# Gated layer: the landing mark of x renamed, the output's weights loaded in two halves behind x

## The chip, the cores and the metric

One core of a Trainium2 chip runs the whole program. TensorE (PE) does the matmuls, ScalarE (ACT), VectorE (DVE) and GpSimd (Pool) the elementwise work, and SyncE (SP) issues the DMAs, all in one queue. The metric is the time of one launch in microseconds of the device, the median of the runs.

## The reference

Three layers follow each other on 4 batches of 576 positions and 512 channels: windowed attention, a feed-forward layer with ReLU ("expert layer" here), and a gated layer. The change lies in the gated layer:

```python
def _moe2_ref(x, w_in, g_ln, w_sg, b_sg, w_out) -> np.ndarray:
    h = x @ w_in
    h = 0.5 * h * (1.0 + np.tanh(c * (h + 0.044715 * h ** 3)))
    u, v = (h[..., :d_ff // 2], h[..., d_ff // 2:])
    ...
    v_n = (v - mu) / np.sqrt(var + 1e-06) * g_ln
    v_s = np.einsum('ts,bsd->btd', w_sg, v_n) + b_sg[None, :, None]
    gated = u * v_s
    return (x + gated @ w_out).astype(np.float32)
```

`w_in` is 512 x 1024, its two halves `wu` and `wv` in the kernel; `w_out` (`wo`) is 512 x 512 and `w_sg` (`ws`) 576 x 576. `w_in` and `w_out` come as 64-bit floats, `w_sg` as 32-bit ones.

## The kernel before

Every product is done in three matmul terms: each operand is split into a rounded part and a rest (`h` and `l`, type F32R), and high x high, low x high and high x low are added up in PSUM. A split (`split`) is one ACT copy, which rounds, and one subtraction on DVE or Pool. The gated layer runs from about 515 us. Its work is cut into **units**: `V`, `U` (the two halves of `x @ w_in`), `S` (the spatial product) for each of the 4 batches, a short unit for the last 64 positions of all batches (`Vt`, `Ut`, "the tail") and `O` for the output's product of each of 9 groups. The order of the units is V0, U0, Vt, V1, U1, V2, U2, V3, U3, Ut, S0, S1, O0, O1, S2, O2, O3, S3 and the other O. The text calls U0 the first U unit, and so on.

A unit of V, U or S multiplies 2 x 2 blocks with seven products of half size in place of eight (`CHAIN`, in the order 1, 2, 6, 5, 7, 3, 4), which needs sums and differences of the blocks ahead (`prep`, `add`; on DVE or Pool) and of the results behind. Behind products 1, 6 and 5 ACT copies PSUM to a tile `te` (`evac`, L1390); products 7 and 3 start only when the copy of 6 and of 5 is done. Behind products 2, 7 and 3 DVE adds PSUM to such a copy (`sum`, L1396); product 4 waits for the sum of 7. ACT's GELU (`use`, L1413) then empties the sum into `u` or `v`, and V's rows are normalized (`norm`: statistics L1429, L1432, L1433 on DVE, a power on Pool, the scaling L1441 on ACT). There are five `te` tiles.

The batches' x lie in DRAM (`x2d`) from the expert layer. `load_x(b)` loads two pieces `xf` of 512 KB each and lets `prep` split seven blocks `bX` from them; `load_tail` does the same for the tail. The 64-bit weights `wo` are loaded in four pieces of 512 KB (`f64`, kc 0 to 3, tile `st`, two of them), turned to 32 bits by one ACT step (L84) and four DVE steps (L89, L91, L93, L96, tile `sc`), and split into `woh` and `wol`. `w_late` does that, then loads and splits a remainder of `ws` (tiles `k`, `b`), then loads the rest of `ws` (tile `wf`) and mixes its blocks (`mixed`, tile `mx`), which overwrite those of `wv`.

The order on each engine is not written by hand. A planner (`Sched`) runs while the program is built: a step is an `Op` with an engine, a guessed duration, a priority and the marks (`need`) that must be set before it. A mark is a name in a table, `done`, with the time at which the planner thinks it set. The planner takes the step that can start first, the priority counted in, and writes its instructions; on the chip each engine then works through its own list in that order. The marks are not on the chip: there, waits follow from what an instruction reads and overwrites. The expert layer sets marks named ("xl", g, p) for its groups g and parts p (in `rest`), and the gated layer's loads set ("xl", b, j).

Of the kernel before, what the change touches and what calls it, by code (L numbers as in the profile page):

```python
# [985 lines left out]
class Phase2:  # L986
# [52 lines left out]
    def open_0(self, sched):  # L1039
# [24 lines left out]
        for b in range(1, B):  # L1064
            self.go(self.load_x(b))
        for z in (self.load_tail(), self.v_tail(), self.u_tail(), self.w_late(), self.finish()):
            self.go(z)
# [51 lines left out]
    def f64(self, w, src, kc):  # L1119
        pri = self.wpri(w) + kc  # L1120
        nd = [("room", "late"), ("xl", 1, 1)] if w == "wo" else []
        yield Op("SP", 500, pri, need=nd, slots=[("st2", 2, ("st2", w, kc))], token=("ld2", w, kc), size=2 ** 19)
# [136 lines left out]
    def load_x(self, b):  # L1259
        pri = self.pri("V", b, -50)  # L1260
        key = "X", b
        fs = []
        for j in range(2):
            nd = [("x2", 2 * b + j)] + ([("P", "V", b - 1, 2)] if b > 1 else [("P", "U", 0, 1)] if b else [])
            o = Op("SP", 500, pri + j, need=nd, take=[("X", 1, ("src", key, j))], token=("xl", b, j), size=2 ** 19)
            yield o
            fs.append(self.get(o.got[0], [128, 4, 256], F32, "xf"))
            self.nc.sync.dma_start(out=fs[j], in_=self.x2d[2 * b + j])
        v = fs[0][:, 0:2], fs[1][:, 0:2], fs[0][:, 2:4], fs[1][:, 2:4]
        if b == 1:  # L1270
            yield Op(None, 0, 0, need=[("b", ("X", B), n) for n in range(3)])
        yield from self.prep(key, v, 2, pri, [("xl", b, 0), ("xl", b, 1)])

# [6 lines left out]
    def load_tail(self):  # L1280
        pri = self.pri("Vt", 0, -50)
        key = "X", B
        o = Op("SP", 500, pri, need=[("x2", G - 1)], take=[("X", 1, ("src", key, 0))], token=("xl", B, 0),
               size=2 ** 19)
# [9 lines left out]
        for n in range(2):  # L1294
            self.go(block(n, x[:, 2 * n:2 * n + 2], [("xl", B, 0)], ("src", key, 0), 3))
        t = yield from self.add(lambda g: self.get(g[0], [128, 2, 256], F32, "tt"), x[:, 2:4], x[:, 0:2], ALU.subtract, 512, pri,
                                take=[("tt", 1, ("tt", key, 2))], need=[("xl", B, 0)])
        self.used(("src", key, 0), 3, self.last)
# [218 lines left out]
    def w_late(self):  # L1517
# [31 lines left out]
        S.done["bdf"] = S.done["bt"] = S.free[self.last] + HOP  # L1549
        pri = self.wpri("ws")  # L1550
        self.W["ws"] = self.W["wv"]
# [208 lines left out]
```

## Time and profile before

| what | value |
|---|---|
| median of 3 runs | 730.87 us (729.82 to 731.5) |
| the profiled execution | 730.48 us |
| its span on the core | 728.6 us |
| PE busy | 706.5 us, 97% |
| DVE, ACT, Pool busy | 529.1, 342.9, 195.2 us |
| granted TensorE clock, mean | 0.994 of full speed |

The span is the time from the first to the last instruction of the core; 1.9 us of the execution lie outside it. A share of busy time is a mean over all stages.

### The profile page before, as it was taken

The numbers are of one execution on the slowest core, as the hardware profiler recorded it, in microseconds if no ns is written. First come the engines' busy times: TensorE is split into PE (matmuls) and PEld (weight loads), VectorE is DVE, ScalarE is ACT, GpSimd is POOL, SyncE is SP. The second block draws the span as 40 slices with busy tenths as digits, with TensorE's granted clock in tenths as the row PEclk, the third lists the DMA queues.
The fourth block names the chain that finished last, engine by engine and source line by source line (L and its number), as shares of the span: only waits on it lengthen the run. The fifth ranks groups of instructions, "written<-read, shape, count | busy, mean of one in ns | idle before, by whom it ended". The sixth has DMA issues, their size and how long they took to land.

```text
span 728.6 us, 17059 instructions
## 1 busy us (share of the span) xinstructions
PE 706.5 (97%) x6734; PEld 676.6 (93%) x6734; DVE 529.1 (73%) x1397; ACT 342.9 (47%) x873; POOL 195.2 (27%) x256
## 2 busy tenths in 40 slices
PE   6889999999999999999999999999999999999997
PEld 3568999999999999999999999999989998999997
DVE  6899989889782673764744737767699969999451
ACT  5887664545532422522424433323478767534110
POOL 2456250334411321312313232000136210333010
PEclk9999999999999999999999999999999999999999
DMA  8564532032221110112022242140531120021433
GB/s 301 173 208 144 178 114 73 28 94 94 78 87 31 56 51 24 49 58 59 20 67 71 55 124 60 58 138 9 180 99 58 54 59 30 30 74 44 145 116 87
DMA packets 49423, 63.36 MB, mean 87 GB/s; under 512 B 9536, under 2 KB 37312, under 8 KB 49344
## 3 DMA queue, kind: packets, MB, share of 16 engines
q1 hardware_dynamic: 49344, 62.28, 27.5%
q8 instruction: 53, 0.87, 0.5%
q14 instruction: 26, 0.21, 0.1%
HBM read 52.83 MB, written 9.44 MB: 85 GB/s over the span
## 4 chain that ended last, share of the span: by engine, by line
PE 75%; DVE 13%; ACT 5%; issue 2%; DMA 2%; POOL 1%; SPq 0%; ACTq 0%; DVEq 0%; POOLq 0%
PE acc L900 25%; PE ps_h L889 25%; PE psO L1661 7%; PE psS L1322 3%; PE s L475 2%; PE psV L1322 2%; PE o L660 1%; PE tps L616 1%; DVE tt L1161 1%; ACT t L526 1%; DVE te L1396 1%; PE o L616 1%; DMA xf<-x2d 1%; PE psU L1322 1%; DVE bX L1153 1%
## 5 line engine op out<-in xcount | busy, mean ns | idle before, releaser
L831 DVE SCALAR_TENSOR_TENSOR hl<-ps_h,hh 128x512 fp32r<-128x512 f32 x72 | 49.7, 690 | 80.3 <-ACT hh L829 79.8
L829 ACT ACTIVATE hh<-ps_h 128x512 fp32r<-128x512 f32 x72 | 43.0, 597 | 117.7 <-PE ps_h L889 117.3
L900 PE MATMUL acc<-hh,w2h 128*128 128x256 f32 x576 | 92.5, 283 | 0.0
L889 PE MATMUL ps_h<-xh,w1h 128*128 128x256 f32 x576 | 91.5, 281 | 0.0
L889 PE MATMUL ps_h<-xh,w1l 128*128 128x256 f32 x576 | 90.0, 278 | 0.0
L889 PE MATMUL ps_h<-xl,w1h 128*128 128x256 f32 x576 | 90.0, 278 | 0.0
L900 PE MATMUL acc<-hh,w2l 128*128 128x256 f32 x576 | 89.9, 278 | 0.0
L900 PE MATMUL acc<-hl,w2h 128*128 128x256 f32 x576 | 89.8, 278 | 0.0
L889 PEld LDWEIGHTS ps_h<-xh,w1h 128*128 128x128 f32 x576 | 77.1, 188 | 1.2 <-issue 1.1
L900 PEld LDWEIGHTS acc<-hh,w2h 128*128 128x128 f32 x576 | 77.3, 189 | 0.1
L900 PEld LDWEIGHTS acc<-hh,w2l 128*128 128x128 f32 x576 | 77.1, 188 | 0.0
L889 PEld LDWEIGHTS ps_h<-xh,w1l 128*128 128x128 f32 x576 | 77.1, 188 | 0.0
L889 PEld LDWEIGHTS ps_h<-xl,w1h 128*128 128x128 f32 x576 | 77.0, 188 | 0.0
L900 PEld LDWEIGHTS acc<-hl,w2h 128*128 128x128 f32 x576 | 76.9, 188 | 0.0
L484 POOL TENSOR_SCALAR_AFFINE_SELECT m<-m 128x256 f32<-128x256 f32 (+1 forms) x88 | 41.9, 482 | 125.2 <-ACT m L565 123.4
L526 ACT ACTIVATE t<-t,sm 128x128 f32<-128x128 f32 x144 | 56.4, 395 | 24.8 <-DVE sm L520 23.8
L534 POOL TENSOR_TENSOR t<-t,sm 128x256 f32<-128x256 f32 x47 | 29.4, 626 | 72.5 <-DVE sm L530 42.0
L1661 PE MATMUL psO<-bG,woh 128*128 128x256 f32 x256 | 45.4, 281 | 0.0
L1322 PE MATMUL psU<-bX,wuh 128*128 128x256 f32 x224 | 40.5, 283 | 2.9 <-ACT te L1390 2.1
L1322 PE MATMUL psV<-wvh,bX 128*128 128x256 f32 x224 | 40.5, 280 | 0.2
L1661 PEld LDWEIGHTS psO<-bG,woh 128*128 128x128 f32 x256 | 39.2, 189 | 0.0
L1322 PEld LDWEIGHTS psU<-bX,wuh 128*128 128x128 f32 x224 | 34.1, 189 | 3.9 <-ACT te L1390 2.5
(259 smaller groups left out, 1657.2 us busy)
## 6 DMA issues: line engine op xcount, KB each, us to landing
st<-in_w SPq DMA_DIRECT2D x24, 512.0 KB, 4.3
x2d<-x SPq DMA_DIRECT2D x18, 256.0 KB, 2.0
xf<-x2d SPq DMA_DIRECT2D x9, 512.0 KB, 4.9
xr<-x2d SPq DMA_DIRECT2D x9, 512.0 KB, 4.4
st<-in_w SPq DMA_DIRECT2D x16, 256.0 KB, 2.6
st<-in_wi SPq DMA_DIRECT2D x8, 512.0 KB, 3.6
out<-xr SPq DMA_DIRECT2D x16, 256.0 KB, 2.4
rq<-in_q SPq DMA_DIRECT2D x28, 128.0 KB, 2.9
```

The lines of the kernel that those rows point to most:

```text
L475: pe.matmul(s.S[h][hs[z], u, c0:c1], q, k, start=True, stop=True, skip_group_check=True)
L484: pool.affine_select(out=out, in_=in_, pattern=pat, compare_op=ALU.is_ge, fill=0.0, base=-1 if up else 0, channel_multiplier=1 if up else -1)
L526: act.activation(out=t[:, h], in_=t[:, h], func=ACTF.Exp, bias=st[:, h:h + 1], scale=-1.0, accum_out=sums[:, h, 0:1])
L534: pool.tensor_tensor(out=t, in0=t, op=ALU.mult, in1=st[:, 6:8].rearrange("p (h o) -> p h o", o=1).to_broadcast([128, 2, 128]))
L616: pe.transpose(spot(e)[:, h], e.t[:, h], ident)
L660: pe.matmul(pair[g][64 * h:64 * h + 64, oc:oc + w], v, s.M[m][k, h, mc:mc + w], start=x == 0, stop=x == len(mm[g]) - 1, skip_group_check=True)
L829: act.activation(out=h, in_=ps, func=ACTF.Relu)
L831: dve.scalar_tensor_tensor(out=l, in0=ps, scalar=0.0, in1=h.bitcast(F32), op0=ALU.max, op1=ALU.subtract)
L889: pe.matmul(ps[:, half], w[:, kc, f], m[:, kc], start=kc == 0 and x == 0, stop=kc == 3 and x == 2)
L900: pe.matmul(accs[half][:, d], w[:, f, ds], m[:, k], start=fi and d == 0 and k == 0 and x == 0, stop=la and k == 1 and x == 2, skip_group_c ...
L1322: pe.matmul(ps[:, e], l[s][:, kt, 128 * e:128 * e + 128], r[m][:, kt], start=fresh and e == 0 and kt == 0 and s == m, stop=kt == 1 and s = ...
L1661: nc.tensor.matmul(ps[:, e], self.wo[s][:, kc, ds], r, start=e == kc == 0 and s == m, stop=kc == 3 and s == 1, skip_group_check=True)
```

## The change

The marks that the gated layer's loads set are renamed from "xl" to "xin". A piece kc of `wo` needs, in place of the mark ("xl", 1, 1), that block 5 of the second batch's x (kc 0 and 1) or of the third's (kc 2 and 3) has been split. And the last part of `w_late`, the loads of `ws`, becomes a generator of its own, `w_gate`, which starts beside `w_late` and doesn't go through its steps first.

```diff
--- before.py
+++ after.py
@@ -1063,7 +1063,7 @@
                 self.go(self.unit(kind, b))
         for b in range(1, B):
             self.go(self.load_x(b))
-        for z in (self.load_tail(), self.v_tail(), self.u_tail(), self.w_late(), self.finish()):
+        for z in (self.load_tail(), self.v_tail(), self.u_tail(), self.w_late(), self.w_gate(), self.finish()):
             self.go(z)
         for b in range(B):
             self.go(self.prep_v(b))
@@ -1118,7 +1118,7 @@
 
     def f64(self, w, src, kc):
         pri = self.wpri(w) + kc
-        nd = [("room", "late"), ("xl", 1, 1)] if w == "wo" else []
+        nd = [("room", "late"), ("b", ("X", 1 + kc // 2), 5)] if w == "wo" else []
         yield Op("SP", 500, pri, need=nd, slots=[("st2", 2, ("st2", w, kc))], token=("ld2", w, kc), size=2 ** 19)
         s = self.sp.tile([128, 512], I64, tag="st", name="st", bufs=2)
         self.nc.sync.dma_start(out=s, in_=src[kc])
@@ -1262,14 +1262,14 @@
         fs = []
         for j in range(2):
             nd = [("x2", 2 * b + j)] + ([("P", "V", b - 1, 2)] if b > 1 else [("P", "U", 0, 1)] if b else [])
-            o = Op("SP", 500, pri + j, need=nd, take=[("X", 1, ("src", key, j))], token=("xl", b, j), size=2 ** 19)
+            o = Op("SP", 500, pri + j, need=nd, take=[("X", 1, ("src", key, j))], token=("xin", b, j), size=2 ** 19)
             yield o
             fs.append(self.get(o.got[0], [128, 4, 256], F32, "xf"))
             self.nc.sync.dma_start(out=fs[j], in_=self.x2d[2 * b + j])
         v = fs[0][:, 0:2], fs[1][:, 0:2], fs[0][:, 2:4], fs[1][:, 2:4]
         if b == 1:
             yield Op(None, 0, 0, need=[("b", ("X", B), n) for n in range(3)])
-        yield from self.prep(key, v, 2, pri, [("xl", b, 0), ("xl", b, 1)])
+        yield from self.prep(key, v, 2, pri, [("xin", b, 0), ("xin", b, 1)])
 
     def prep_v(self, b):
         yield Op(None, 0, 0, need=[("va", b, 0), ("va", b, 1)] + [("P", "U", B - 1, 4) if b == 1 else ("P", "S", b - 1, 1) if b else ("wsl", 1)])
@@ -1280,7 +1280,7 @@
     def load_tail(self):
         pri = self.pri("Vt", 0, -50)
         key = "X", B
-        o = Op("SP", 500, pri, need=[("x2", G - 1)], take=[("X", 1, ("src", key, 0))], token=("xl", B, 0),
+        o = Op("SP", 500, pri, need=[("x2", G - 1)], take=[("X", 1, ("src", key, 0))], token=("xin", B, 0),
                size=2 ** 19)
         yield o
         x = self.get(o.got[0], [128, 4, 256], F32, "xf")
@@ -1292,9 +1292,9 @@
             S.done["b", key, n] = S.free[self.last] + HOP
             self.used(tok, c, self.last)
         for n in range(2):
-            self.go(block(n, x[:, 2 * n:2 * n + 2], [("xl", B, 0)], ("src", key, 0), 3))
+            self.go(block(n, x[:, 2 * n:2 * n + 2], [("xin", B, 0)], ("src", key, 0), 3))
         t = yield from self.add(lambda g: self.get(g[0], [128, 2, 256], F32, "tt"), x[:, 2:4], x[:, 0:2], ALU.subtract, 512, pri,
-                                take=[("tt", 1, ("tt", key, 2))], need=[("xl", B, 0)])
+                                take=[("tt", 1, ("tt", key, 2))], need=[("xin", B, 0)])
         self.used(("src", key, 0), 3, self.last)
         self.go(block(2, t, [], ("tt", key, 2), 1))
 
@@ -1547,7 +1547,9 @@
             yield from self.split(self.bt[n][:, :, 0:64], self.bt[n][:, :, 64:128], src, 128, pri)
         yield from self.split(self.kn[:, 0:64], self.kn[:, 64:128], y[:, 4], 64, pri)
         S.done["bdf"] = S.done["bt"] = S.free[self.last] + HOP
-        pri = self.wpri("ws")
+
+    def w_gate(self):
+        nc, S, pri = self.nc, self.sched, self.wpri("ws")
         self.W["ws"] = self.W["wv"]
         for e in range(2):
             o = Op("SP", 1000, pri, need=[("b", ("X", B - 1), n) for n in range(7)], take=[("X", 1, ("wsf", e))], token=("wsl", e),
```

The order on SP, the queue of all DMAs, from the small constants of the gated layer on: `xf<-x2d_65` is the tail's x, 59 and 60 are the second batch's, 61 and 62 the third's.

```order
 L1111 DMA bb<-in_bsg 128x576
 L1112 DMA g_7349<-in_g 128x4
-L1124 DMA st<-in_wo 128x512 x2
 L1287 DMA xf<-x2d_65 128x1024
 L1268 DMA xf<-x2d_59 128x1024
 L1268 DMA xf<-x2d_60 128x1024
-L1124 DMA st<-in_wo 128x512
+L1124 DMA st<-in_wo 128x512 x2
 L1268 DMA xf<-x2d_61 128x1024
 L1268 DMA xf<-x2d_62 128x1024
```

The first two pieces of `wo` move behind the tail's and the second batch's x.

DVE from the three sums of V0 to the first two of U0, before:

```order
L1396 TENSOR_TENSOR te<-te,psV 128x512 x3
L1429 BN_STATS bs<-v 128x6
L89 TENSOR_SCALAR sc<-sc 128x512
L91 TENSOR_SCALAR sc<-sc 128x512
L1429 BN_STATS bs<-v 128x6
L93 SCALAR_TENSOR_TENSOR sc<-st,sc 128x512
L1432 BN_AGGR ag<-bs 128x2 x2
L1433 TENSOR_SCALAR ag<-ag 128x2
L96 SCALAR_TENSOR_TENSOR sc<-st,sc 128x512
L1396 TENSOR_TENSOR te<-te,psU 128x512
```

and in the changed kernel:

```order
L1396 TENSOR_TENSOR te<-te,psV 128x512 x3
L1429 BN_STATS bs<-v 128x6 x3
L1432 BN_AGGR ag<-bs 128x2 x2
L1433 TENSOR_SCALAR ag<-ag 128x2
L1429 BN_STATS bs<-v 128x6
L1432 BN_AGGR ag<-bs 128x2 x2
L1433 TENSOR_SCALAR ag<-ag 128x2
L1161 TENSOR_TENSOR tt<-xf 128x512
L1396 TENSOR_TENSOR te<-te,psU 128x512
```

The four steps on `sc` have left this place; the statistics of both halves of V0 and the tail's difference `tt<-xf`, which was Pool's, stand ahead of U0's first sum.

DVE at the end of V3 and the beginning of U3 in the changed kernel (the three sums of V3 and U3 are the lines L1396):

```order
L1153 TENSOR_TENSOR wol<-sc,woh 128x512
L1161 TENSOR_TENSOR mx<-wf 128x256
L1396 TENSOR_TENSOR te<-te,psV 128x512
L1161 TENSOR_TENSOR mx<-wf,mx 128x256
L1161 TENSOR_TENSOR mx<-wf 128x256
L1153 TENSOR_TENSOR wvl<-wf,wvh 128x256
L1153 TENSOR_TENSOR wvl<-mx,wvh 128x2x256
L1161 TENSOR_TENSOR mx<-wf,mx 128x256 x2
L1153 TENSOR_TENSOR wvl<-wf,wvh 128x2x256
L1161 TENSOR_TENSOR mx<-wf 128x256
L1396 TENSOR_TENSOR te<-te,psU 128x512
```

Before, the last piece of `wo` (`wol`) stood in V2, and the mixing (`mx`) began behind the first sum of U3; now the last `wol` and the first `mx` stand in front of V3's last sum.

## Rows read from the trace of the kernel before

**Rows 1.** The page's first part: engine, busy us (share of the span), instructions.

```profile
PE 706.5 (97%) x6734; PEld 676.6 (93%) x6734; DVE 529.1 (73%) x1397; ACT 342.9 (47%) x873; POOL 195.2 (27%) x256
```

**Rows 2.** The timeline of PE from 515 to 645 us (start us, us, engine, instruction [idle before <-releaser]).

```profile
531.90 0.51 PE L1322 MATMUL psU<-bX,wuh 128*128 128x256 f32 x2 [1.41 <-ACT te L1390]
...
535.47 0.50 PE L1322 MATMUL psU<-bX,wuh 128*128 128x256 f32 x2 [0.39 <-DVE te L1396]
...
559.11 0.51 PE L1322 MATMUL psU<-bX,wuh 128*128 128x256 f32 x2 [0.71 <-ACT te L1390]
...
582.51 0.50 PE L1322 MATMUL psU<-bX,wuh 128*128 128x256 f32 x2 [0.43 <-DVE te L1396]
...
583.99 0.28 PE L1322 MATMUL psV<-wvh,bX 128*128 128x256 f32 x1
...
609.92 0.28 PE L1322 MATMUL psS<-wvh,bN 128*128 128x256 f32 x1
...
612.17 0.51 PE L1322 MATMUL psS<-wvh,bN 128*128 128x256 f32 x2 [0.49 <-DVE bN L1153]
...
615.01 0.38 PE L1322 MATMUL psS<-wvh,bN 128*128 128x256 f32 x1 [0.97 <-ACT te L1390]
...
636.93 1.10 PE L1591 MATMUL psN<-J,te 128*128 128x64 f32 x8 [0.28 <-ACT te L1586]
...
641.09 0.39 PE L1322 MATMUL psS<-wvh,more 128*128 128x256 f32 x1 [1.17 <-DVE te L1396]
```

**Rows 3.** The chain that ended last, 514 to 600 us: start us, us, what.

```profile
521.38 7.51 DMA xf<-x2d
...
594.50 2.84 PE psU L1322 x24
```

**Rows 4.** The timeline of ACT, 524 to 616 us.

```profile
530.21 0.63 ACT L1413 ACTIVATE u<-te 128x512 f32<-128x512 f32 x1 [2.05 <-DVE te L1396]
...
531.27 0.58 ACT L1390 ACTIVATE te<-psU 128x512 f32<-128x512 f32 x1
...
599.73 0.81 ACT L1441 ACTIVATE v<-v,ag 128x512 f32<-128x512 f32 x1
...
611.29 1.14 ACT L1413 ACTIVATE v<-te 128x512 f32<-128x512 f32 x2
```

**Rows 5.** The timeline of DVE in the first U unit.

```profile
528.01 0.98 DVE L1433 TENSOR_SCALAR ag<-ag 128x2 f32<-128x2 f32 x1
...
528.91 0.68 DVE L96 SCALAR_TENSOR_TENSOR sc<-st,sc 128x512 int32<-128x512 int32 x1
...
529.51 0.67 DVE L1396 TENSOR_TENSOR te<-te,psU 128x512 f32<-128x512 f32 x1
...
533.02 1.79 DVE L1153 TENSOR_TENSOR bX<-tt,bX 128x512 fp32r<-128x512 f32 x1
```

**Rows 6.** The timeline of Pool in the same stretch.

```profile
527.64 1.32 POOL L1161 TENSOR_TENSOR tt<-xf 128x512 f32<-128x512 f32 x1 [11.88 <-DMA xf<-x2d]
...
532.97 1.29 POOL L1153 TENSOR_TENSOR wol<-sc,woh 128x512 fp32r<-128x512 f32 x1 [2.82 <-DVE ag L1432]
```

**Rows 7.** The timeline of SP: DMA issues.

```profile
519.01 0.90 SPq L1124 DMA_DIRECT2D st<-in_wo  x2
...
520.48 0.33 SPq L1287 DMA_DIRECT2D xf<-x2d  x1
```

**Rows 8.** Stretches: us, busy of each engine (instructions), PEclk, DMA share, GB/s.

```profile
523.00:524.00 1.00, 1.00 (x11) 1.00 (x10) 0.42 (x1) 0.64 (x1) 0.00 (x0) 1.00 1.03 415
```

**Rows 9.** Stretches of 10 us from 570 to 610, one of them and the sum.

```profile
590.00:600.00 10.00, 10.00 (x86) 10.00 (x86) 5.93 (x14) 4.55 (x11) 2.59 (x4) 1.00 0.01 2
...
sum 40.00, PE 39.45 PEld 38.84 DVE 31.43 ACT 28.37 POOL 9.34; mean PE 9.86 PEld 9.71 DVE 7.86 ACT 7.09 POOL 2.34
```

**Rows 10.** The timeline of DVE in the two first S units.

```profile
622.57 0.69 DVE L1396 TENSOR_TENSOR te<-te,psS 128x512 f32<-128x512 f32 x1
...
640.37 0.67 DVE L1396 TENSOR_TENSOR te<-te,psS 128x512 f32<-128x512 f32 x1
```

## The prediction

> **What bounds the kernel now.** The page's busy line comes first: PE is busy 706.5 us of the span [rows 1], so all that any reordering can win is PE's idle time. The waits of PE in order of time say where it lies in the part that the change touches. There are eight from 515 us on: two in the first U unit (1.41 and 0.39 us), one in the second U unit (0.71), one in the third (0.43), two in the first S unit (0.49, 0.97) and two in the second (0.28, 1.17), 5.85 us in all [rows 2]; the two rows there without a wait are the starts of the fourth V and of the first S unit. Behind 643 us PE never waits. Each wait costs a little more than its bracket says: by the chain, 24 matmuls take 2.84 us without a wait [rows 3], 0.118 us each, and a matmul lasts 0.28 us, so the queue has to fill again, about 0.2 us a time. The gain is thus at most some 7.5 us, 1%, and a change of order can also open new waits of the same kind.
>
> What ends the waits in the U units is read on ACT and DVE. Product 7 waits until ACT has copied product 6 out of PSUM. That copy started at 531.27, behind a GELU (`u<-te`) that started only at 530.21, because DVE's sum (`te<-te,psU`) before it started at 529.51 [rows 4, 5]. DVE was late since it works in order and had a piece of the output's weights in hand: its last step (L96) started at 528.91 [rows 5]. The second wait (0.39) is DVE's too. Its sum stood behind a split of 533.02 that took 1.79 us, where the like steps around it take 0.67 or 0.68, and in just that time Pool ran its own step of the same weights, 532.97 to 534.26 [rows 5, 6].
>
> **The change, part by part.** *The mark's new name.* Where x lands, the scheduler sets the mark only as the load is issued, and the users of x are generated after that, so they read the right value under either name. Only the weights `wo` asked for ("xl", 1, 1) from outside, found the expert layer's mark of the same name, long set, and so were put ahead of x. The renaming by itself removes and adds no instruction: 0 us.
>
> *The loads.* Two of the four 512 KB pieces of `wo` were issued at 519.01, the tail's x at 520.48 [rows 7]. In the new order they come behind the tail's and the first pair's x. The mark is the planner's, not a semaphore: on the chip they go out right behind those loads, and 1 MB only changes places. The queue moved 415 GB/s there [rows 8], so the tail's x, for which Pool waited until 527.64 [rows 6], lands 1 MB / 415 GB/s = 2.5 us earlier, at 525.1; the pair's, 528.9 by the chain [rows 3], at 526.4.
>
> *First U unit.* DVE loses the weights' four steps here (two short ones, two of 0.60 from start to start) and gets the tail's difference from Pool (0.60) and a normalization's statistics that stood behind the sum (two of 0.60 and 0.4 of small ones). By count that is even. What goes is a hold-up: a step on two numbers took 0.98 us, to the end of that difference on Pool (528.96) [rows 5, 6]; I count 0.8 of it. The sum starts at 528.7. ACT: GELU at 529.4, then one normalization step (the nearest row is 0.81 long [rows 4], next start 0.71 later), the copy of product 6 at 530.7 to 531.25. Product 7 starts at 531.3 instead of 531.90: 0.6 us won. With no weights on Pool and DVE the second wait goes with its refill, 0.65, and the small one at product 3, 0.15: **-1.4 us** at the unit's end. Bounds: 0 (the tail's x late by over 2 us, so that ACT waits for it) and -2.2 (both waits gone wholly).
>
> *Second and third V and U units.* Here two of the weights' pieces are converted as before, in other places, and the other two move into the third U and the fourth V unit. A product is 12 matmuls, 1.42 us. From the second V unit's start at 541.3 eleven products end at 556.9, where product 7 of the second U unit could start. ACT's copy for it stands behind a GELU that waits for DVE's sum, and DVE has from 552.6 (V's last GELU; V's last sum waits for ACT's first step on the weights) two statistics, two weight steps and a split, five of 0.60, then the sum, to 556.4. GELU, one weight step and the copy end at 558.1. Product 7 starts at 558.15 against 559.11: of 1.4 us won 0.95 are left. If Pool holds up one split on DVE the way row 533.02 shows (about 0.65 of it in the way), it starts at 558.8, and 0.3 are left. The third U unit goes alike: DVE has two statistics, two short weight steps, a split and a difference ahead of the sum, ACT two splits ahead of the copy, so product 7 waits some 1.1 us where it did not, while the 0.43 goes. The fourth V unit then starts at 583.35 without a hold-up and at 584.0 with one, against 583.99 [rows 2]. I take the later: **+1.4 us**, all that was won. The bounds are +0.7 and +2.6 (a hold-up of 0.65 in each of two more units).
>
> The split of 533.02 and Pool's step ended within 0.6 us of each other, and the split took 1.1 us more than its like [rows 5, 6]: one seems to wait for the other. By the order three more 512-wide steps go to Pool. If each takes its full 1.29 us out of DVE's path, the sum below ends 3.9 us later: that is a rival. The Trainium skill (SBUF — State Buffer, Who interferes with whom) says it as a rule: a GpSimd instruction that reads SBUF and a VectorE one with two SBUF inputs shut each other out for a whole instruction, whichever starts first. The rows at 533 agree with it.
>
> *Fourth V unit to the tail.* Between 570 and 610 us DVE is busy 31.4 of 40 us, least from 590 to 600, 5.93 [rows 9], idle 8.6 in all. Two pieces of weights now come in, each 0.8 + 3 x 0.6 = 2.6 us, 5.2 together. The spatial weights' loads stand ahead of their small remainder's now, and their mixing is taken up during V's end instead of after 598: it fills the hole at 590. V's own small gaps (0.5 us in all) should go. **-0.4 us** at the first S unit, 609.5 against 609.92 [rows 2]; bounds 0 and -1.0.
>
> *First S unit.* Its first wait (DVE's split) goes, since the blocks are split some 4 us sooner. The second can't go: three of the GELU outputs take tiles that the tail's product frees as it ends, six GELUs run from 611.29 at 0.57 us or a little less each [rows 4], and the copy that PE waits for follows them. From the tail's end at 609.8 that is 613.5 to 614.1 with a split left ahead of them, so product 6 starts at 614.1 against 615.01: **-0.5 us** more. Bounds 0 and -1.0.
>
> *Second S unit.* The 1.17 us wait is DVE's backlog: the sum started at 640.37 [rows 10], though PE had ended its product before 636.65 (636.93 less the wait of 0.28 [rows 2]). From the like sum of the first S unit, 622.57 [rows 10], DVE worked 17.8 us with hardly a pause. In the new order the second batch's blocks are split before the first of these sums, and 21 steps stand between the two, most of 0.60 us, about 14 us: the sum is ready some 2 us before PE asks. **-1.4 us** with its refill. The 0.28 stays (ACT's copy still stands behind a split). Bounds 0 and -1.9.
>
> Behind it PE has no wait to lose. **Sum:** -1.4 + 1.4 - 0.4 - 0.5 - 1.4 = -2.3 us. The profiled execution took 730.48 us, 1.9 outside its span; it becomes 728.2, and the median, 730.87, becomes **728.5 us**, 0.32% faster.
>
> **Rivals.**
> *Given back.* The hold-ups in the second and third U unit cost 2.6 instead of 1.4, and the second S unit's backlog shifts rather than goes (+0.7): 2.3 - 1.9 = 0.4 us won, 730.5, no change that can be told. For it speaks that the waits there come from ACT's and DVE's order, not from their load, and that DVE has work added in the third; against it that the S units gain from DVE work that is really taken forward.
> *DVE too late at the first S unit: slower.* The 5.2 us of weights stand ahead of V's sums in an in-order queue. If none of the idle 8.6 us takes them up, since DVE idles waiting for PE and ACT and not by choice, the mixing and the S unit come 5.2 us later: -1.4 + 5.2 = +3.8, 734.7. It decides from 1.4 + 1.5 = 2.9 us of the 5.2 unabsorbed. Three hold-ups by Pool of 1.29 us each end on the same side: -2.3 + 3.9 = +1.6, 732.5.
> *More goes.* No hold-up in the U units and every S wait gone: -1.4 - 0.4 - 1.0 - 1.9 - 0.5 = -5.2, 725.7. The waits in brackets allow it; the GELUs' wait for the tail's tiles speaks against it.
>
> **How the numbers follow.** A measurement tells 0.2%, 1.5 us, from no change. The forecast with its own bounds (-1.5 to -4) has 0.52, more 0.10, given back 0.24, slower 0.14 (0.08 for the queue, 0.06 for Pool). So faster 0.62, same 0.24, slower 0.14. The range reaches from the case where more goes to just past no change, 725.9 to 731.6: it leaves out most of the slower cases and a little below, 2 in 10.
>
> **What would show it.** The tail's x lands by 525.5, and the first U unit loses no more than 0.9 us to waits. PE then waits at product 7 of the second and the third U unit, 1 to 2 us each, released by ACT's copy. No S product waits for a split by DVE; product 6 of the first S unit still waits about 1 us for ACT; product 4 of the second no longer waits. The prediction is wrong if waits in the second and third U unit pass 2 us each, if the first S product itself waits, or if the 1.17 us wait stays.

## Result and profile after: 0.8% slower

The changed kernel took 736.57 us (median of 4 runs, 735.94 to 738.75) where the kernel before took 731.18 beside it: ratio 1.0082, 95% interval 1.0057 to 1.0107. Measured once more beside the experiments it took 734.79 (6 runs), ratio 1.0056, 1.0037 to 1.0076. It is slower, by 4 to 5.5 us; 728.5 was predicted.

The page's first part, to be held against [rows 1]:

```profile
PE 711.2 (96%) x6734; PEld 681.5 (92%) x6734; DVE 527.4 (72%) x1394; ACT 341.8 (46%) x873; POOL 197.1 (27%) x259
```

The same 6734 matmuls keep PE busy for 4.7 us more: some of them ran slower. The profiled execution took 738.75 us (span 737.0). PE's waits in order of time, against [rows 2] (start us, us, engine, instruction, and in brackets the wait ahead and its releaser):

```profile
532.91 0.53 PE L1322 MATMUL psU<-bX,wuh 128*128 128x256 f32 x2 [1.81 <-ACT te L1390]
...
548.19 0.38 PE L1322 MATMUL psV<-wvh,bX 128*128 128x256 f32 x1 [0.73 <-ACT te L1390]
...
563.28 0.50 PE L1322 MATMUL psU<-bX,wuh 128*128 128x256 f32 x2 [1.97 <-ACT te L1390]
...
586.46 0.50 PE L1322 MATMUL psU<-bX,wuh 128*128 128x256 f32 x2 [1.88 <-ACT te L1390]
...
612.07 0.51 PE L1322 MATMUL psU<-bX,wuh 128*128 128x256 f32 x2 [1.11 <-DVE te L1396]
...
623.51 0.39 PE L1322 MATMUL psS<-wvh,bN 128*128 128x256 f32 x1 [0.92 <-ACT te L1390]
...
646.73 1.10 PE L1593 MATMUL psN<-J,te 128*128 128x64 f32 x8 [0.57 <-ACT te L1588]
```

The 1.17 us of the second S unit and the split's wait in the first are gone. In their place product 7 of the first, second and third U unit waits 1.81, 1.97 and 1.88 us for ACT's copy, product 6 of the second V unit 0.73, and product 4 of the fourth U unit 1.11.

The lists of ACT, DVE and Pool say why. ACT around the first and the third of these rows:

```profile
530.44 0.63 ACT L1150 ACTIVATE bX<-tt 128x512 fp32r<-128x512 f32 x1 [1.91 <-DVE tt L1161]
531.04 0.63 ACT L1413 ACTIVATE u<-te 128x512 f32<-128x512 f32 x1
531.57 0.80 ACT L1441 ACTIVATE v<-v,ag 128x512 f32<-128x512 f32 x1
532.28 0.57 ACT L1390 ACTIVATE te<-psU 128x512 f32<-128x512 f32 x1
...
561.60 0.63 ACT L1413 ACTIVATE u<-te 128x512 f32<-128x512 f32 x1 [2.31 <-DVE te L1396]
562.13 0.61 ACT L1150 ACTIVATE woh<-sc 128x512 fp32r<-128x512 f32 x1
562.65 0.58 ACT L1390 ACTIVATE te<-psU 128x512 f32<-128x512 f32 x1
```

The copy stands behind a GELU (`u<-te`) that needs DVE's sum, and behind one step more. ACT itself stood idle ahead of it, 1.91 us in the first unit for the difference `tt`, which DVE does just ahead of the sum, and 2.31 us in the second for the sum. Ahead of that sum on DVE:

```profile
528.58 1.23 DVE L1433 TENSOR_SCALAR ag<-ag 128x2 f32<-128x2 f32 x1
...
530.33 0.67 DVE L1396 TENSOR_TENSOR te<-te,psU 128x512 f32<-128x512 f32 x1
...
559.19 1.77 DVE L96 SCALAR_TENSOR_TENSOR sc<-st,sc 128x512 int32<-128x512 int32 x1
560.89 0.67 DVE L1396 TENSOR_TENSOR te<-te,psU 128x512 f32<-128x512 f32 x1
```

and on Pool at those times:

```profile
528.49 1.30 POOL L1153 TENSOR_TENSOR bX<-xf,bX 128x512 fp32r<-128x512 f32 x1
...
558.85 1.57 POOL L1153 TENSOR_TENSOR bX<-xf,bX 128x512 fp32r<-128x512 f32 x1 [0.81 <-ACT bX L1150]
```

Each time a DVE step that is 0.17 or 0.68 us long elsewhere takes over 1 us more. It ends with a Pool step (529.81 and 529.79) or half a microsecond behind it (560.96 and 560.42). The loads did what was foreseen: the tail's x was issued at 520.80 and landed 4.1 us later, at 524.9.

Behind the wait of 1.81 us the granted clock (the seventh number of a stretch, behind the busy times of PE, weight loads, DVE, ACT and Pool) is half for 3.5 us:

```profile
532.00:533.00 1.00, 0.09 (x1) 0.10 (x1) 0.35 (x2) 1.00 (x3) 0.00 (x0) 1.00 0.00 0
533.00:534.00 1.00, 1.00 (x6) 1.00 (x7) 0.00 (x0) 1.00 (x3) 0.00 (x0) 0.64 0.00 0
534.00:535.00 1.00, 1.00 (x7) 1.00 (x6) 0.00 (x0) 0.75 (x2) 0.00 (x0) 0.50 0.00 0
...
537.00:538.00 1.00, 1.00 (x11) 1.00 (x10) 0.44 (x1) 0.55 (x2) 0.00 (x0) 1.00 0.00 0
```

PE starts 6 or 7 matmuls in such a microsecond where it starts 11 at the full 2.4 GHz. The same stands behind the waits of 1.97 and 1.88. Before, the clock is 1.00 all the way from 525 to 640 us.

By stage, from the starts of the units (us, each against the same stretch of the kernel before):

| stretch | before | changed, first profile | changed, second profile | predicted |
|---|---|---|---|---|
| first U unit | 12.22 | +1.22 | -0.39 | -1.4 |
| second V to third U unit | 41.28 | +6.52 | +6.71 | +1.4 |
| fourth V unit to the tail's end | 25.93 | +1.05 | -0.56 | -0.4 |
| the first two S units | 33.16 | -0.91 | -1.17 | -1.9 |
| from the first V to the first O unit | 127.88 | +7.88 | +4.60 | -2.3 |

(The first V unit and the tail's V, 15.3 us together, are the same in all.) The second profile is that of the repeated run, after_again. The program is the same in both; what parts them in the first U unit and behind the fourth V unit is told under fill and after_again.

### The profile page after: what moved, and what is told of

Its sections match the earlier page's. It is cut to its first block, busy times and chain, and to the rows that moved or that the text cites. A ratio compares the mean times of both kernels' runs of the same rounds, so it can differ in the third digit from the quotient of the medians.

```text
span 737.0 us, 17063 instructions
## 1 busy us (share of the span) xinstructions
PE 711.2 (96%) x6734; PEld 681.5 (92%) x6734; DVE 527.4 (72%) x1394; ACT 341.8 (46%) x873; POOL 197.1 (27%) x259
## 4 chain that ended last, share of the span: by engine, by line
PE 81%; DVE 8%; ACT 5%; issue 3%; DMA 1%; POOL 0%; SPq 0%; ACTq 0%; DVEq 0%
PE ps_h L889 26%; PE acc L900 25%; PE psO L1663 7%; PE psV L1322 5%; PE psU L1322 4%; PE psS L1322 3%; PE s L475 2%; PE o L660 1%; PE tps L616 1%; ACT t L526 1%; PE o L616 1%; DVE sc L93 1%; PE tps L660 1%; DVE sc L96 1%; PE psS L1331 1%
## 5 line engine op out<-in xcount | busy, mean ns | idle before, releaser
L1322 PE MATMUL psU<-bX,wuh 128*128 128x256 f32 x224 | 43.8, 297 | 6.8 <-ACT te L1390 5.7
L1322 PEld LDWEIGHTS psU<-bX,wuh 128*128 128x128 f32 x224 | 37.2, 205 | 7.7 <-ACT te L1390 6.2
```

Of the source, the lines that this page charges most:

```text
L1322: pe.matmul(ps[:, e], l[s][:, kt, 128 * e:128 * e + 128], r[m][:, kt], start=fresh and e == 0 and kt == 0 and s == m, stop=kt == 1 and s = ...
```

## The experiments

Fifteen other kernels were run, and the changed one once more. All ratios are to the kernel before, run beside them; differences between kernels are taken from the ratios (1% is 7.3 us) and are uncertain by 0.2 to 0.25%.

| run | what it is | us | ratio, 95% interval |
|---|---|---|---|
| after_again | the changed kernel | 734.79 | 1.0056 (1.0037 to 1.0076) |
| fill | changed, 12 idle matmuls in each wait | 735.14 | 1.0063 (1.0045 to 1.0081) |
| copy_twice | before, one ACT copy more | 730.84 | 1.0007 (0.9995 to 1.0018) |
| rename | before + part 1 | 742.70 | 1.0163 (1.0146 to 1.0180) |
| wo_alone | before + part 2 | 752.25 | 1.0301 (1.0281 to 1.0321) |
| gate_old | before + part 3 | 731.17 | 1.0004 (0.9991 to 1.0016) |
| gate_alone | before + parts 1 and 3 | 733.77 | 1.0052 (1.0034 to 1.0070) |
| no_pool | changed, edit P | 732.09 | 1.0022 (1.0009 to 1.0035) |
| early800 | changed, edit E | 732.40 | 1.0027 (1.0013 to 1.0040) |
| no_pool_early | changed, P and E | 729.46 | 0.9991 (0.9979 to 1.0004) |
| b_no_pool | before, P | 730.20 | 0.9991 (0.9978 to 1.0005) |
| bearly800 | before, E | 730.33 | 0.9999 (0.9987 to 1.0011) |
| b_no_pool_early | before, P and E | 728.18 | 0.9967 (0.9954 to 0.9980) |
| gate_both | before + part 3, P and E | 725.47 | 0.9921 (0.9904 to 0.9939) |
| after_less2 | changed, eight DVE steps left out | 731.51 | 1.0007 (0.9994 to 1.0020) |
| gate_less2 | before + part 3, the same eight left out | 728.78 | 0.9957 (0.9942 to 0.9972) |

Part 1 is the marks' new name, part 2 the new mark that the output's weights ask for, part 3 the generator `w_gate`.

### Is it the clock?

```diff
-            ps = banks[bk]
+            ps, fill = banks[bk], 12 * (kind == "U" and P == 7 and b < 3)
+            z = fill and self.get(S.stock["bank"][S.free_of("bank")[0][1]], [128, 2, 256], F32, "fill")
+            for m in range(fill):
+                self.nc.tensor.matmul(z[:, 0], self.W["wu"][0][:, a, 0, 0:128], self.X[key, c][0][:, 0], start=True, stop=True)
```

fill. 

> The changed kernel with 12 more matmuls (their result is never read) written in front of product 7 of the first three U units, where TensorE waited 1.81, 1.97 and 1.88 us for ACT's copy; every other instruction stands where it stood. Twelve matmuls of 0.118 us fill 1.42 us of each wait, so product 7 can't start sooner, but the engine isn't idle for so long. Theory A (the granted clock falls to half after these waits, and that is worth some 1.6 us each): the clock stays at 1.00 from 525 to 595 us, the waits left are about 0.4, 0.55 and 0.45 us, and the time is about 5 us under the changed kernel's, 731.5, within 0.3% of the kernel before. Rival B (the waits alone make the loss, and the clock falls for another reason): the clock falls as before in the same places, and the time stays at 736.5.

The clock did stay at 1.00 from 525 to 700 us, and yet the time did not come down to 731.5: 1.0063 lies between the two measurements of the changed kernel. PE in this run (L1399 is the sum's line here):

```profile
534.14 0.50 PE L1322 MATMUL psU<-bX,wuh 128*128 128x256 f32 x2 [0.40 <-ACT te L1393]
...
573.52 0.39 PE L1322 MATMUL psV<-wvh,bX 128*128 128x256 f32 x1 [0.65 <-ACT te L1393]
...
609.55 0.50 PE L1322 MATMUL psU<-bX,wuh 128*128 128x256 f32 x2 [1.12 <-DVE te L1399]
```

The stretch from the second V to the third U unit is shorter by 2.4 us than in the second profile, which has two falls there; a wait of 0.65 us stands in the third V unit, where that profile has none. The wait of 1.12 us in the fourth U unit has nothing to do with the clock: the first profile has it too, behind three falls. There DVE and Pool hold each other, and the same two lists gave one outcome in the first profile and in fill, another in the second profile. In the first profile DVE's `tt` and `mx`, which stand ahead of the sum, are long:

```profile
607.42 1.07 POOL L1161 TENSOR_TENSOR tt<-k 128x256 f32<-128x256 f32 x1 [0.82 <-POOL wvl L1153]
...
607.81 1.23 DVE L1161 TENSOR_TENSOR tt<-v 128x512 f32<-128x512 f32 x1
...
608.96 1.52 DVE L1161 TENSOR_TENSOR mx<-wf,mx 128x256 f32<-128x256 f32 x1
```

In the second profile Pool's step is long and DVE's are short:

```profile
606.26 2.95 POOL L1161 TENSOR_TENSOR tt<-k 128x256 f32<-128x256 f32 x1 [0.76 <-POOL wvl L1153]
...
606.64 0.69 DVE L1161 TENSOR_TENSOR tt<-v 128x512 f32<-128x512 f32 x1
...
607.25 0.42 DVE L1161 TENSOR_TENSOR mx<-wf,mx 128x256 f32<-128x256 f32 x1
```

With the first outcome the stretch from the fourth V unit to the tail's end is 1.6 us longer, 1.11 of it this wait. From the first V to the first O unit fill takes 132.0 us: 3.8 less than the first profile (three falls, the same outcome) and 0.5 less than the second (two falls, the other outcome). So the falls cost something in these profiles; the medians, whose difference is uncertain by 2 us, show none of it and can't exclude up to some 2 us. Theory A fell as an account of the loss: without a fall there the profile is still 4.1 us behind the kernel before, and the time 0.63%.

copy_twice (one line, in `evac`: the copy of product 6 of the first U unit is done again). 

> The kernel before with one ACT copy more: the copy of product 6 in the first U unit is done twice, so that product 7's wait there grows from 1.41 to about 1.9 us; nothing else moves. Theory A (a wait of that length is followed by some 3.5 us at half clock): the granted clock falls to 0.50 behind that wait, and the time grows by 0.5 for the copy and 1.6 for the clock, 2.1 us, to about 733. Rival B (a wait costs what its bracket says): no fall of the clock, +0.5 us, 731.5.

The wait became 1.96 us and the clock fell behind it (0.50 at 534 and 535). At the first U unit's end the profile is 1.37 us behind the kernel before, at the first O unit 0.81, for the next waits of 0.71 and 0.39 shrank or went; over 12 runs +0.07% is left (-0.05 to +0.18). Theory A's 2.1 us did not come; the 0.5 of B did, though not for its reason, since the clock fell.

after_again. 

> The changed kernel once more, to have it beside the others on one chip and to see whether the clock falls in the same places in another profiled execution. Theory A (waits, and the clock behind them): 735.5 to 737, the same waits of 1.8 to 2.0 us at product 7 of the first three U units, and the clock at 0.50 behind two or three of them. Rival B (the falls are accidents of one execution): the waits as before, no fall between 525 and 600 us, and a time under 735.5.

The waits are the same, and the first of them shows that the fall isn't bound to happen:

```profile
533.22 0.51 PE L1322 MATMUL psU<-bX,wuh 128*128 128x256 f32 x2 [1.81 <-ACT te L1390]
...
561.99 0.50 PE L1322 MATMUL psU<-bX,wuh 128*128 128x256 f32 x2 [1.98 <-ACT te L1390]
...
585.33 0.50 PE L1322 MATMUL psU<-bX,wuh 128*128 128x256 f32 x2 [1.79 <-ACT te L1390]
```

Behind 533.22 the clock stays at 1.00, behind the other two it is 0.50. So the first U unit gives the price of one fall with the same wait ahead: 13.44 us with it, 11.83 without, 1.6 us.

### Which part?

```diff
-        nd = [("room", "late"), ("xl", 1, 1)] if w == "wo" else []
+        nd = [("room", "late"), ("b", ("X", 1 + kc // 2), 5)] if w == "wo" else []
```

wo_alone. 

> The kernel before with the second part of the change alone: the pieces of the output's weights ask for block 5 of the second and the third batch's x. The order up to the fourth V unit is that of the changed kernel; the loads of the spatial weights stay where they were. Theory A (the U units make the loss): three waits of 1.8 to 2.0 us at product 7 of the first three U units with the clock at half behind each, +8 us by the fourth V unit, and the S units' waits of the kernel before on top: 737 to 738. Rival C (the spatial weights' mixing, taken forward, makes the loss): 731 to 732.

The waits of the U units were as foreseen (1.81, 1.97, 1.79 us; the clock fell behind the last two alone), the S units were not:

```profile
624.57 0.58 PE L1322 MATMUL psS<-wvh,bN 128*128 128x256 f32 x1 [7.64 <-ACT wvh L1150]
...
637.60 0.58 PE L1322 MATMUL psS<-wvh,bN 128*128 128x256 f32 x1 [3.69 <-ACT bN L1150]
```

With the weights' pieces later, the remainder of `ws` and the loads behind it in `w_late` come later too: those of `wf` were issued at 598.01 against 582.12 before. Part 3 undoes just that; without it part 2 costs 3%.

gate_alone. 

> The changed kernel with the old mark for the output's weights, so that two of their pieces stand ahead of x again: the third part of the change alone. Theory A: no wait over 1.5 us at a product 7 of the U units, the clock stays at 1.00, and the second S unit loses its wait of 1.17 us: 729 to 730.5. Rival C (the spatial weights' mixing makes the loss): about 736.

It came out at 733.77, and it wasn't what its text calls it: it keeps the new names, so all four pieces of `wo` go by the old mark. Two more kernels part the two.

rename. 

> The kernel before with the first part of the change alone, the marks' new name. The prediction put it at nothing. By the order of the program the third piece of the output's weights is turned to 32 bits earlier, in front of the second V unit's copies, and the second U unit's order changes. If that is what cost the run with the first and the third part its 0.5%, this one has the waits of that run's U units (1.24 and 0.63 us in the second, 1.01 and 1.06 in the third) and 733 to 734; if the third part cost it, this one is at 730 to 731.

gate_old. 

> The kernel before with the third part alone, the spatial weights' loads in a generator of their own, and the old marks. The order is that of the kernel before up to the fourth V unit. If the prediction's S units were right (the wait of 1.17 us in the second S unit goes, the splits of the first come earlier), 728.5 to 730; if the third part is what cost, 732 or more, with waits for the small remainder's blocks, which now come behind the mixing, in the first S unit.

The new name alone costs 1.6%, far more than either text allowed: the U units have the waits that were named (1.24 and 0.63, 1.01 and 1.04 us), and the first S unit waits 4.91 us for a split. By the code, the third and fourth piece of `wo` had been asking for the mark as the gated layer set it anew; under the new name they find the old one. In the changed kernel the output's weights don't ask for that name any more, so this doesn't act there. Part 3 alone changes nothing in the time that can be told: the wait of 1.17 us goes and the first two S units are 0.85 us shorter, but the units ahead of them are 0.75 longer. Part 2 beside part 3 thus costs 1.0056 - 1.0004, 0.5%, 3.8 us.

### Is it Pool's hold on DVE, or ACT's order?

Edit P, in `by`, and edit E, in the planner's `run`:

```diff
-        return {"DVE": self.nc.vector, "POOL": self.nc.gpsimd}[o.eng]
+        return {"DVE": self.nc.vector, "POOL": self.nc.gpsimd}["DVE" if len(o.alt) > 1 and ("P", "V", 0, 4) in self.sched.done and ("P", "U", 3, 4) not in self.sched.done else o.eng]
...
-                key = (start + TRADE * min(max(op.pri, -99), 99), op.pri, n)
+                key = (start + TRADE * min(max(op.pri, -99), 99) - 800 * (op.eng == "ACT" and (op.token or " ")[0] == "e"), op.pri, n)
```

no_pool. 

> The changed kernel with the splits and differences that Pool did from the first V unit's end to the third U unit's end and the fourth's begin done by VectorE, in the same order of the program; Pool keeps the powers and the tail's half-height splits. Theory H (a step of VectorE is held until Pool's ends, and that makes the long waits): the steps of 1.2 to 1.8 us on VectorE (528.58, 545.02, 559.19, 563.98, 581.24, 607.81) fall to their usual 0.2 or 0.7, each for one step more of 0.6; the sums come about 0.5 us earlier, the waits at product 7 fall to about 1.3 us, the clock stays up, 732 to 733. Rival O (it is the order on ScalarE, and the work of VectorE, whoever holds whom): 13 steps of 0.6 us more on VectorE, the waits stay or grow, 736.5 to 739.

Theory H had it in the U units. The two held steps are short again:

```profile
528.89 0.17 DVE L1433 TENSOR_SCALAR ag<-ag 128x2 f32<-128x2 f32 x1
...
556.95 0.69 DVE L96 SCALAR_TENSOR_TENSOR sc<-st,sc 128x512 int32<-128x512 int32 x1
```

and product 7 waits about half as long, with the clock at 1.00 up to the S units:

```profile
532.37 0.51 PE L1322 MATMUL psU<-bX,wuh 128*128 128x256 f32 x2 [0.96 <-ACT te L1390]
...
559.96 0.51 PE L1322 MATMUL psU<-bX,wuh 128*128 128x256 f32 x2 [0.77 <-ACT te L1390]
...
581.59 0.50 PE L1322 MATMUL psU<-bX,wuh 128*128 128x256 f32 x2 [0.87 <-ACT te L1390]
```

early800. 

> The changed kernel with one number more in the planner: ScalarE's copies of a product out of PSUM count as startable 0.8 us earlier than they are, so that they are written in front of the GELU, the normalization and the splits that the planner thought it could start just ahead of them. Theory O (the waits at product 7 come from ScalarE working its list in order: it idles 1.9 to 2.3 us for VectorE's sum with the copy behind the GELU, though product 6 has long ended): the waits of 1.81, 1.97 and 1.88 us go, and the clock stays at 1.00; 5.7 us of waits, 0.6 of refills and some 3 of the clock against some 2 that come back elsewhere, 729 to 730.5. Rival H (VectorE's sums are late, and the next product waits for them instead): product 4 waits where product 7 did, 1 us or more each, 733 to 735.

In the first and third U unit theory O had it: waits of 0.51 and 0.75. In the second the rival had it:

```profile
560.29 0.50 PE L1322 MATMUL psU<-bX,wuh 128*128 128x256 f32 x2 [1.13 <-ACT te L1390]
...
563.83 0.38 PE L1322 MATMUL psU<-bX,wuh 128*128 128x256 f32 x1 [1.88 <-DVE te L1396]
```

There L96 stood ahead of the sum, held by Pool to 1.77 us. 732.40 lies between the two expectations. Both edits leave a loss in the first S unit: with P, product 6 waits 1.75 us there for ACT's copy, with E the product for the last 64 positions (`psT`) waits 1.60 us for DVE's split of a remainder block `b`, and the clock falls behind either.

bearly800. 

> The same number in the kernel before. Theory O: its waits for a copy by ScalarE (1.41 and 0.71 us in the U units, 0.97 in the first S unit) shrink or go, 727.5 to 729. Rival H: product 4 waits for VectorE's sums instead, 730 to 731.

b_no_pool. 

> The kernel before with the edit of the run that took the splits and differences off Pool: from the first V unit's end to the third U unit's end and the fourth's begin VectorE does those that Pool did (11 steps), in the same order of the program. The kernel before has three steps of VectorE of 1.66 to 1.79 us there (533.02, 547.51, 580.08), the changed kernel five of over 1.2 and two more of 1.2 on two numbers. Theory H (what the change lost it lost to Pool's hold-ups, which fell on the sums): 729.5 to 731 here, since these three lie where little waits for them, and the changed kernel without Pool's steps (732.1) is within 1.5 us of this one. Rival O (the change's order of work is worse whoever holds whom): this one gains the same as the changed kernel did, some 2.5 us, 728, and the distance between the two stays at 4 us.

no_pool_early. 

> The changed kernel with both edits: no splits and differences on Pool in the U units, and ScalarE's copies counted as startable 0.8 us earlier. If each edit took away a loss of its own, the copies come before the GELU and no step is held: the waits at product 7 go under 0.5 us and the clock stays up up to the S units, 729 to 730.5, level with the kernel before or just under. If both took away the same loss (the copy's wait for the late sum), no more than either alone: 731.5 to 732.5.

b_no_pool_early. 

> The kernel before with both edits, to see whether the change is worth anything once its U units are rid of these waits. If the change's gains in the S units are real (the wait of 1.17 us in the second one gone), this one is 0.5 to 1.5 us behind the changed kernel with both edits: 730 to 731. If they are given back, it is ahead: 728 to 729.5.

gate_both. 

> The kernel before with the third part and both edits (no splits and differences on Pool in the U units, ScalarE's copies counted as startable 0.8 us earlier). If the third part's gain in the S units is real, the wait of 1.70 us in the second S unit of the kernel before with both edits goes, and this is 1 to 2 us under its 728.2; if it is given back at the first S unit, 728 to 729.5.

In the changed kernel P brings 0.34%, E 0.29%, both 0.65%: each took away a loss of its own, as the first case of no_pool_early has it. In the kernel before neither alone brings anything that can be told. With E rival H had it (product 4 waits 0.72 and 1.06 us for DVE's sum in the second and third U unit); with P the time is the one that theory H gave, but its distance to the changed kernel with P, 0.31% or 2.3 us, lies between H's 1.5 and O's 4. Both edits bring 0.33% and put the kernel before ahead of the changed one (728.18 against 729.46). With part 3 added they bring 0.79%, more than its text allowed: 725.47 us, the fastest of all and under both kernels, with three waits over 0.2 us left from the first U unit to the second S unit:

```profile
561.85 0.50 PE L1322 MATMUL psU<-bX,wuh 128*128 128x256 f32 x2 [0.27 <-DVE te L1396]
...
578.42 0.50 PE L1322 MATMUL psU<-bX,wuh 128*128 128x256 f32 x2 [0.91 <-ACT te L1390]
...
633.98 0.32 PE L1593 MATMUL psN<-J,te 128*128 128x64 f32 x1 [0.54 <-ACT te L1588]
```

So part 3 is worth something (0.46%) once the waits ahead of it are gone. But part 2 costs with both edits no less, 0.9991 - 0.9921, 0.7%, than without, 0.5%. It is another loss, though. From the second V to the third U unit the changed kernel takes 47.99 us in its second profile, 6.6 more than gate_old; with both edits it takes 41.50, and gate_both 41.30. In the U units the loss is gone. With the edits the changed kernel is behind gate_both by 0.9 us from the fourth V unit to the tail's end and by 3.7 in the first two S units, where PE waits for the remainder's blocks `b`:

```profile
615.94 0.39 PE L1576 MATMUL psT<-bN,b 128*128 128x256 f32 x1 [0.72 <-DVE b L1153]
618.23 0.58 PE L1578 MATMUL psT<-vt,b 128*128 128x256 f32 x1 [1.54 <-DVE b L1153]
```

The clock fell at the second of these waits (0.50 at 619 and 620). The remainder comes behind the output's weights, which part 2 delays: the last five of its loads were issued at 589.56 us here and at 571.88 in gate_both. So hold-ups and ACT's order account for the loss in the U units, and part 2 has a second price, the late remainder, which shows once these units are fast.

### Is it the moved work of DVE?

```diff
-            for n in z:
+            for n in z if w != "wo" or kc > 1 else ():
                 j.bits(n)
```

after_less2. 

> The changed kernel without VectorE's four steps on each of the first two pieces of the output's weights (eight steps, left out; these weights come out wrong, everything else stands in its place). Theory D (the moved steps of VectorE make the loss, since they now stand ahead of the second U unit's sum): the wait of 1.97 us at product 7 of the second U unit falls under 1 us, the others stay, and the time falls by 2 to 3.5 us, to 731 to 732.5. Rival O (the order on ScalarE and Pool around them): the waits stay within 0.4 us of what they were, 734 to 735.

gate_less2. 

> The control: the kernel with the third part alone, without the same eight steps of VectorE, which stand there in the first V and the first U unit. Theory D: it gains less than the changed kernel does, since these steps lie where TensorE waits for little: the first U unit's wait of 1.18 us shrinks by 0.5 to 0.9 and its 0.40 stays, 730 to 731. If it gains as much as the changed kernel, the steps' place is not what costs.

In the changed kernel the wait of 1.97 us is gone altogether, the others stay:

```profile
533.47 0.50 PE L1322 MATMUL psU<-bX,wuh 128*128 128x256 f32 x2 [1.81 <-ACT te L1390]
...
581.62 0.50 PE L1322 MATMUL psU<-bX,wuh 128*128 128x256 f32 x2 [1.87 <-ACT te L1390]
```

The eight steps cost 0.49% there, 3.6 us, and theory D had the place: the sum of the second U unit starts without them at 557.45, in time, and the copy behind it too. But the control gained as much, 0.47%, where D allowed under 0.15%: the first U unit falls from 12.04 to 10.54 us. By its own rule D isn't shown. The profiles put the steps' cost at 2.0 us in the old place and at 4.0 in the new (127.60 to 125.62 us from the first V to the first O unit, and 132.48 to 126.88 less 1.6 for a fall of the clock behind 581.62 that this execution was spared), the medians can't tell the two apart, and without the steps part 2 still costs 0.5%. Of that the profiles place 1.29 us in the first U unit, where 10.54 us would do and the changed kernel takes 11.83: what took the steps' place there, the split on Pool beside the normalization and the normalization ahead of the copy, seems to give the gain back; no run takes these two out alone. They place 1.49 us from the second V to the third U unit, where product 7 of the third still waits 1.87 us, and take 1.29 back behind the fourth V unit. How the rest of part 2's cost divides stays open.

## Why the prediction was wrong

The step that failed is the term "second and third V and U units, +1.4", bounds 0.7 and 2.6; it measured +6.5 and +6.7. Its mechanism was right: product 7 waits for ACT's copy behind a GELU and a late sum. For the second U unit it had a wait of 1.9 us (556.9 to 558.8), and 1.97 was measured, though the hold-up fell on a weight step and not on a split. What was missing: 0.7 of the third U unit's wait (1.1 against 1.88 and 1.79), product 6 of the second V unit (0.73 and a refill of 0.2), and the clock, which the prediction left out: two falls of some 1.5 us each in place. Without the falls the term would still have been wrong: fill has +4.4 here. The term's own addition is off as well: 1.1 us for 0.43 costs 0.67, which puts the fourth V unit at 584.36 and the term near +1.8.

**First U unit, -1.4.** Wrong in its mechanism; the -0.39 of the profile without a fall lies within its bounds. DVE lost the weights' steps as foreseen, but "what goes is a hold-up" did not hold: Pool, relieved of the difference, took the tail's split instead, and the same kind of step waited again, 1.23 us instead of 0.98. With Pool kept out (no_pool) the unit is 1.24 us shorter than before.

**Fourth V unit to the tail, -0.4.** Right in the second profile (-0.56); in the first a wait of 1.11 us for DVE's sum made it +1.05. Which of the two comes depends on who holds whom, and the sum had no term for that.

**S units, -1.9.** Right in kind: no wait for a split, 0.92 us at product 6, none at product 4 of the second. Half in size, -0.9 and -1.2. The first unit won 0.3 and 0.5 us of the 0.5; the second won 0.6 and 0.65 of the 1.4, for part of the 1.17 us comes back as waits for ACT's copies, 0.23 and 0.43 at an earlier product and 0.57 and 0.67 at `psN` against the 0.28 of [rows 2].

**The renaming, 0 us.** It is nothing in this change, but only because part 2 replaces the mark: by itself it costs 1.6%.

**The rivals.** "DVE too late: slower" came to 734.7, near what was measured, by luck. Its place was wrong (the first S unit; it was the U units), and so was its condition: its work was to stand ahead of V's sums in the last units, while what told was work ahead of U's first sum. The Pool rival (732.5) was nearer in kind: without Pool's steps 0.34% came back, 2.5 us of the 4. The two had 0.14 between them, too little, as the term above held both causes at their mildest.

**What was to show it.** The sign that the waits pass 2 us each was set too far out: 1.97 and 1.88 stayed under it while the kernel was already slower.

## What to carry to other kernels

Work moved out of one full stretch has to be priced in the stretch where it lands, step by step on each in-order engine and with the holds between DVE and Pool counted anew, for they move with it. Let a planner put the copy that the next product waits for ahead of steps that wait for another engine, and try edits together: P and E brought little each in the kernel before, with part 3 they brought 0.79%. A wait that the kernel closes is no gain until the next one in line is looked at. Two profiles of one program can differ by 1.6 us in one stretch, by a fall of the clock or by who holds whom, so a difference of that size between two kernels' profiles needs the medians beside it.

## What the runs showed of the hardware

The granted clock fell to 0.50, 1.2 GHz, for some 3.5 us behind 12 of the 18 waits of PE between 1.54 and 1.98 us that these profiles hold from 525 us on, within or behind each of the three longer ones (3.69, 4.91, 7.64), and no fall began behind one of 1.41 us or less. The same wait of 1.81 us in the first U unit was followed by a fall in one execution of the changed kernel and not in another. The Trainium skill (TensorE: Matmul & The Clock Gate, HAM oscillation — how this bites in real kernels) tells of a kernel whose clock falls at each wait for data, and counts half of the time at the low level as lost. The fall here costs about that in place, 1.6 of 3.5 us; what of it stays at the end, the medians of fill do not tell.

A DVE step on two numbers with one input, 0.17 us long, took 1.23 us beside a split on Pool that had started 0.09 us ahead, and 0.17 again while Pool stood idle. In all profiles together 32 such steps of the gated layer started while a 512-wide Pool step ran: 24 of them ended 0.02 to 0.03 us behind that step's end, having taken 0.39 to 1.23 us, and the other eight, which started in about its last 0.3 us, were not held. The Trainium skill (SBUF — State Buffer, Who interferes with whom) says that such a step with scalars can lock Pool out or be locked out like one with two inputs, if it runs in a mode that takes both ports. The rows agree, though none shows the mode.

The hold goes both ways, and not always the same way: in the fourth U unit Pool's `tt<-k` took 1.07 us in one execution of the changed kernel and 2.95 in the other, DVE's two steps beside it 1.23 and 1.52, or 0.69 and 0.42.
